# Moving loads, one batch's stores and a store stream around DMA transposes in a fused attention and Fourier-mixing kernel

## The chip, the cores and the metric

The kernel runs on one core of a Trainium2 chip. The metric is device time in microseconds (us): the median of the runs before is 414.62 us (three runs, 414.11 to 414.83). A core has five engines that work through their own instruction lists in order: TensorE (PE in the profile; its weight loads are PEld), VectorE (DVE), ScalarE (ACT), GpSimd (POOL) and SyncE (SP). DMA transfers are issued by an engine's queue and move data while the engines compute; here SP issues the stores and the DMA transposes, POOL the loads.

## The reference

For each of 8 batches and 8 heads, with 576 rows and head dimension 64, the first half is linear attention with exponential features of width 256, and the second half mixes its result along rows and columns with a Fourier transform, normalises, and applies a two-layer network:

```python
def phi(x):
    proj = np.einsum('bhsd,df->bhsf', x, w_phi)
    proj = proj - np.max(np.abs(proj), axis=-1, keepdims=True)
    return np.concatenate([np.exp(proj), np.exp(-proj)], axis=-1)
q_p, k_p = phi(q), phi(k)
kv = np.einsum('bhsf,bhsd->bhfd', k_p, v)
z = np.sum(k_p, axis=2)
attn = np.einsum('bhsf,bhfd->bhsd', q_p, kv) / (np.einsum('bhsf,bhf->bhs', q_p, z)[..., None] + 1e-06)
x = attn, heads joined to (8, 576, 512)
u = x + real(fft over rows and columns of x)
un = (u - mean(u)) / sqrt(var(u) + 1e-06)      # over the 512 columns
out = u + relu(un @ w_ch1) @ w_ch2              # 512 -> 2048 -> 512
```

Inputs and output are float32; the products run in bfloat16.

## The kernel before, in words

Batches are software-pipelined: while the two-layer network of batch b runs, attention and mixing of batch b+1 and the key and query features of batch b+2 are computed between its steps. There is no planner at run time. The order is the string `PLAN` (lines 23 to 37): each letter names a stream, a Python generator that emits some instructions and yields; `step` (line 1345) runs the generator of that letter to its next yield. Every engine executes its instructions in the order in which they are emitted, so the place of a letter fixes the place of its instructions on each engine's list and on each DMA queue.

The streams that matter here, with b the batch:

- `F` (`forward`, line 1200), 68 steps a batch: the network. `hidden(0, 256)` multiplies the first 256 columns of the transposed input `UT` with `W1b` (line 1211, tile `psf`), two 128-row blocks numbered c = 0 and c = 2; `output(c)` multiplies with `W2b` (line 1228, tile `pso`); then `hidden(256, 576)` for blocks 1, 3 and 4. At the end of an `output(c)` DVE adds the result into the tile `X` (line 1234) and the store of block c is issued on SP (`store`, line 1184): one DMA of 256 KB for block 2 and for block 3, four of 128 KB for blocks 0 and 1 together, two for block 4.
- `M` (`mixing`, line 989): per head the key-value product (`keyvalue`, line 842, tile `kv`), `combine` (tile `pn_`, with POOL writing `X` at line 973), then the Fourier mixing, which ends with adds into `X`.
- `N` (`normalise`, line 1100), five steps, blocks in the order 0, 2, 1, 3, 4: DVE takes the statistics (line 1155), ACT writes the centred block `UN` (line 1131), and SP issues a DMA transpose of it into `UT` (line 1148).
- `S` (`scaled`, line 593): POOL multiplies V with its weights, two instructions for each pair of heads (`scale_v`, line 441, tiles `VCn`, `VCp`).
- `K`, `Q`, `V` (lines 1289 to 1309): loads of k, q, v issued on POOL (line 258). `Q` has three steps: four DMAs of 64 KB (`QS01`), one of 256 KB (`QS23`), two for the last block (`QS4`). `K` has two: `KS4` (64 KB) and `KS` (512 KB). `V` has three: two DMAs `VS4` (32 KB each), then two of 256 KB.
- `A` and `B` (`turn_q`, `turn_k`, lines 380 to 398): DMA transposes of q and k on SP, after the loads.

`X` has three buffers; each holds 5 blocks of C + 1 = 513 float32 in every partition, 512 of them used. Three set-up tiles (`gc`, `gs`, `ga`) use the same buffers at the start. The staging tiles of k, q and v have one buffer each, so a load waits until the transposes of the batch before have read the tile.

In the program each tile starts at a multiple of 32 bytes in its partition. A buffer of `X` has 5 x 513 x 4 = 10,260 bytes and takes 10,272; behind the three buffers lie `HT`, `R`, `CEO`, `UN` and `UT`, and `UN` starts at byte 213,408, which is 160 past a multiple of 256.

Of the kernel before, what the change touches and what calls it, by code (L numbers as in the profile page):

```python
# [12 lines left out]
F32 = mybir.dt.float32  # L13
# [9 lines left out]
PLAN = (  # L23
    "CYCCZYCYGGTRTTGZZGTYZWRTJTSRJGRJYSTPTSPKTTPJMJRTSSKMYMBMPTQPTPQVTMZTMQTMMTPCMMMTTMTHDYAMMYHHDHHKYYVD"
    "YDTMTMHTKZMRMSRTYMTTMNYMRVTYQNNMTNTSMNMBFFFRFFNUFNFSMFWFUNRUFQUMTPSFFMNTFPSMTFTNUPYFQMUFPPTVMFTPMTPF"
    "FMMFTTFMFAUTFMMFFMFMFMFMFFKRFPDFFTTTFFDVFFDRFTFFVDFFKTSRFQVFFFFMFFMTFRFFFFFSMTMFFMRTFFMSTMFTFNNMFMQF"
    "PTMMFTFSFMPTFFPTTPMFFFFMFSNBFMFPTQMFFAFMNPFTFMNMFFMFFMMFTTFFURMFFVFRMFFSTFFMFFMFVFTTPFFFFRFPDFFFTPFF"
    "FFFVDDRFFFQFDTMTFFQTSMKFFFMFFFKMRMFTTTMMFNNFFMMFMQFMFFSSMTFMTFFFNFSTPPMFTFMBFPTFPAMFFFMFNTFKMMFFFNFM"
    "FMFFMFFUMQMFFVMFFFTTPFFFFMTFFRFTTFFVFFFRFFRFDFFFFDFDFFDPTFMFTTFFFFMKFRFTMSFMRFFMFTSPMFNTMPQNSFFFFQMM"
    "MMTTTFFBMSFFFFTPMTFSFFMFFMTPVMFFFFMTPNFFNNMMMFFMAFFFMUFMFKMFFFMFFTTDTTFRFFSFFFFRVFFTMFFFFFRPTFFDFFFD"  # L30
    "RFFFTDFMFVKTPFFFFFMTMBQMFFRSFMFTSTSTMMKFFFNNSFMMFMMFTFMFPTMKFFFFPTPMTFFMFFFNMFTPPMFFFTNFQMNMVFFMFQMF"
    "MFFMUFFMFFVMAFFFFTTTTFDRFRFFTFSFFFFMRFFQFFFDFFTFFFDFFRFVDFTFMFFTTMFFMFFMFRSMFQTTTMFTQFNFMSVFFMFFTNPM"
    "MFMSTPMTFFFFSMTPPMFTFFMPPFBAFMFPFMFNNFMMVFMFMFFFMTTFRMNUFFFFFMRFFFMFFFSTFFMFFPTFFTFFFDDFFFRFTFFFDFDV"
    "RFFFMFTTFFMFMTMFRFFSMFFSFMTTNTFFMFNMMFFFMMFTFMPSTFNFFFPTFMFFTMPFFFFMPSPMFFTMFFPFTMNFFFNMFMFFFUMFMFMF"
    "FFFMFFMFMFFFFFDFFDFFFFFDFFFDFMFFFMFMFFMMFFMFNFMNFFFFFFMFFFFFMNFFFMFFNFFFFFFFFFFFFFFFNUFFFFFFFFFFFFFF"
    "FFFFFFFFFFFFFFFFFFFFFFFFFFFFFFFFFFFFF"
)


# [1 line left out]
def kernel(  # L41
# [29 lines left out]
    xpool = ctx.enter_context(tc.tile_pool(name="xpool", bufs=3))  # L71
# [18 lines left out]
    def load_ffn_weights(b):  # L90
# [310 lines left out]
    made, mixed, folds, turned_u, scale_of = {}, {}, {}, {}, {}  # L401
# [493 lines left out]
        yield  # L895

    def first_heads():
        X = xpool.tile([128, 5, C + 1], F32, tag="X", name="X")
        R = fpool.tile([128, 3, 2, 512], F32, tag="R", name="R")
        CEO = fpool.tile([128, 3, 2, 2, 128], BF16, tag="CEO", name="CEO")  # L900
        HI = HIS[0]
        folds[0] = folded(X, R, HI)

        def combine(heads_, ps):
            for e, h in enumerate(heads_):
                for c in range(5):
# [14 lines left out]

        kvh = {}
        for pr in PAIRS:
            for e in range(2):
                kvh[2 * pr + e] = keyvalue(0, 2 * pr + e)
                yield
        for h in (0, 1, 6, 7):
            ps = pb.tile([128, 1, 512], F32, tag="pb", name="pn_")
            combine((h,), ps)
            yield  # L930
        for h in (4, 2):
            ps = pj.tile([128, 2, 512], F32, tag="pj", name="pn_")
            combine((h, h + 1), ps)
            yield
        return X, R, CEO, HI

    def heads(b):
        if b == 0:
            return (yield from first_heads())
        KPp, KPn, K4p, K4n, VCp, VCn, E2 = made[b]  # L940
        X = xpool.tile([128, 5, C + 1], F32, tag="X", name="X")
        R = fpool.tile([128, 3, 2, 512], F32, tag="R", name="R")
        CEO = fpool.tile([128, 3, 2, 2, 128], BF16, tag="CEO", name="CEO")
        HI = HIS[b % 2]
        folds[b] = folded(X, R, HI)

        held = []

        def combine(h, kvh):
            pn_ = pj.tile([128, 2, 512], F32, tag="pj", name="pn_")  # L950
            for c in range(5):
                for i, QP in enumerate((QPHP, QPHN)):
                    nc.tensor.matmul(  # L953
                        pn_[:, i, 65 * c:65 * c + 65], lhsT=QP[:, h, 128 * c:128 * c + 128],
                        rhs=kvh[:, i, :], start=True, stop=True,
                    )
            Av = pn_[:, 0, 0:325].rearrange("p (c n) -> p c n", n=65)
            Bv = pn_[:, 1, 0:325].rearrange("p (c n) -> p c n", n=65)
            tg = work.tile([128, 5, D + 1], F32, tag="tg", name="tg")
            nc.vector.tensor_tensor(  # L960
                out=tg[:], in0=Bv, in1=E2[:, h, :].unsqueeze(2).to_broadcast([128, 5, D + 1]),
                op=ALU.mult,
            )
            if h % 2 == 0:
                held.append(work.tile([128, 2, 5, D + 1], F32, tag="cb", name="cb"))
            cb = held[-1]
            nc.vector.tensor_tensor(out=cb[:, h % 2], in0=Av, in1=tg[:], op=ALU.add)  # L967
            if h % 2 == 0:
                return
            rd = small.tile([128, 2, 5, 1], F32, tag="rd", name="rd")  # L970
            nc.vector.reciprocal(out=rd[:], in_=cb[:, :, :, D:D + 1])  # L971
            at = D * (h - 1)
            nc.gpsimd.tensor_tensor(  # L973
                out=X[:, :, at:at + 2 * D].rearrange("p c (e d) -> p e c d", e=2),
                in0=cb[:, :, :, 0:D], in1=rd[:].to_broadcast([128, 2, 5, D]), op=ALU.mult,
            )
# [223 lines left out]
    def forward(b):  # L1200
        U, UT = turned_u[b]
# [22 lines left out]
        def output(c):  # L1224
            at = PLACE[c]
            po = pb.tile([128, C], F32, tag="pb", name="pso")
            for hh in range(NHH):
                nc.tensor.matmul(  # L1228
                    po[:], lhsT=HT[:, hh, at:at + 128], rhs=W2b[:, hh, :],
                    start=(hh == 0), stop=(hh == NHH - 1),  # L1230
                )
                if hh % 2 and hh < NHH - 1:
                    yield
            nc.vector.scalar_tensor_tensor(  # L1234
                out=U[:, c, 0:C], in0=po[:], scalar=scale_of[b, c], in1=U[:, c, 0:C],
                op0=ALU.mult, op1=ALU.add,
            )
# [22 lines left out]
        for g in range(2):  # L1260
            nc.vector.scalar_tensor_tensor(
                out=U[0:64, 4, 256 * g:256 * g + 256], in0=po[64 * g:64 * g + 64, 0:256],
                scalar=scale_of[b, 4][0:64], in1=U[0:64, 4, 256 * g:256 * g + 256],
                op0=ALU.mult, op1=ALU.add,
            )
        store(b, U, 4)
        yield
        if b < B - 1:
            return
        for at in (0, 256):  # L1270
            po = pb.tile([128, 256], F32, tag="pb", name="pso")
            for hh in range(NHH):
# [58 lines left out]
    def fold_later(b):  # L1331
# [62 lines left out]
```

## Time and profile before

| | |
|---|---|
| median of the runs | 414.62 us (414.11 to 414.83) |
| the profiled execution, its own time | 413.11 us |
| its span, first to last instruction | 411.3 us |
| busy: PE, DVE, ACT, POOL | 390.4, 319.4, 303.6, 214.9 us |
| granted TensorE clock | 0.999 |
| DMA packets moved | 42.71 MB |

Times in the profile count from the start of the span. In a timeline row the columns are: start, length, engine, line, operation, output tile <- input tiles, shapes, number of instructions merged, and in brackets the idle time of the engine just before with what the profile takes to have ended it. A `q` behind an engine's name (`SPq`) marks the issuing of a DMA. A wait for several semaphores is put down to the one that came last by the profile's account.

### The profile page before, as it was taken

The numbers are of one execution on the slowest core, as the hardware profiler recorded it, in microseconds if no ns is written. First come the engines' busy times: TensorE is split into PE (matmuls) and PEld (weight loads), VectorE is DVE, ScalarE is ACT, GpSimd is POOL, SyncE is SP. The second block draws the span as 40 slices with busy tenths as digits, with TensorE's granted clock in tenths as the row PEclk, the third lists the DMA queues.
The fourth block names the chain that finished last, engine by engine and source line by source line (L and its number), as shares of the span: only waits on it lengthen the run. The fifth ranks groups of instructions, "written<-read, shape, count | busy, mean of one in ns | idle before, by whom it ended". The sixth has DMA issues, their size and how long they took to land.

```text
span 411.3 us, 10509 instructions
## 1 busy us (share of the span) xinstructions
PE 390.4 (95%) x4165; PEld 258.7 (63%) x4194; DVE 319.4 (78%) x662; ACT 303.6 (74%) x617; POOL 214.9 (52%) x279
## 2 busy tenths in 40 slices
PE   7898899989999989999899999999999999999995
PEld 3574477535856568566766577556856586657564
DVE  5979887999699877798589888888799768866102
ACT  7988999658958886688868887799768886444350
POOL 8998695774466753807658383649362343201000
PEclk9999999999999999999999999999999999999999
DMA  7999969998574798664964959857782141106202
GB/s 221 218 165 159 184 103 181 88 120 129 101 120 58 68 165 137 77 98 77 137 97 58 155 103 143 88 75 117 114 101 53 33 97 21 26 3 114 60 25 65
DMA packets 108674, 42.71 MB, mean 104 GB/s; under 512 B 82769, under 2 KB 103633, under 8 KB 108625
## 3 DMA queue, kind: packets, MB, share of 16 engines
q0 software_dynamic: 46272, 16.60, 37.3%
q1 hardware_dynamic: 61905, 25.11, 33.2%
q8 instruction: 33, 0.54, 0.5%
q10 hardware_dynamic: 448, 0.33, 0.3%
q14 instruction: 16, 0.13, 0.1%
HBM read 36.77 MB, written 9.44 MB: 112 GB/s over the span
## 4 chain that ended last, share of the span: by engine, by line
PE 77%; DVE 13%; DMA 3%; ACT 3%; POOL 2%; issue 2%; POOLq 0%; DVEq 0%; ACTq 0%
PE psf L1211 30%; PE pso L1228 20%; PE kv L851 4%; PE psD L1033 2%; PE pso L1254 2%; DMA UT<-UN 2%; PE pu L1085 2%; PE idle L1325 2%; PE psq L520 2%; PE psh L561 2%; PE psk L466 1%; DVE cb L967 1%; DVE MK L486 1%; DVE tg L960 1%; DVE R L867 1%
## 5 line engine op out<-in xcount | busy, mean ns | idle before, releaser
L1211 PE MATMUL psf<-UT,W1b 128*128 128x320 bf16 (+1 forms) x1024 | 141.1, 286 | 2.7 <-DVE MQ L528 1.3
L1228 PE MATMUL pso<-W2b,HT 128*128 128x512 bf16 x467 | 117.0, 379 | 1.8 <-issue 0.6
L1211 PEld LDWEIGHTS <-W1b 128*128 128x128 bf16 x1024 | 94.7, 98 | 30.5 <-issue 3.9
L1216 ACT ACTIVATE HT<-psf 128x320 bf16<-128x320 f32 x128 | 53.9, 444 | 25.6 <-PE psf L1211 19.5
L1228 PEld LDWEIGHTS <-HT 128*128 128x128 bf16 x496 | 45.1, 98 | 43.2 <-issue 0.4
L973 POOL TENSOR_TENSOR X<-cb,rd 128x640 f32<-128x640 f32 x28 | 35.1, 1253 | 52.4 <-DVE rd L971 29.5
L441 POOL TENSOR_TENSOR VCn<-VS,VCn 128x512 bf16<-128x512 bf16 x28 | 29.9, 1066 | 43.1 <-ACT VCn L436 36.7
L528 DVE TENSOR_REDUCE MQ<-psq 128x8 f32<-128x1024 f32 (+1 forms) x32 | 34.3, 1088 | 17.3 <-PE psq L520 17.0
L1234 DVE SCALAR_TENSOR_TENSOR X<-pso,rs,X 128x512 f32<-128x512 f32 x31 | 23.0, 743 | 28.2 <-PE pso L1228 28.0
L1218 ACT ACTIVATE HT<-psf 128x512 bf16<-128x512 f32 x64 | 37.3, 602 | 6.4 <-PE psf L1211 6.2
L486 DVE TENSOR_REDUCE MK<-psk 128x8 f32<-128x1024 f32 x28 | 33.8, 1210 | 1.4 <-ACT KPn L472 1.4
L472 ACT ACTIVATE KPp<-psk 128x1024 bf16<-128x1024 f32 x28 | 28.8, 1027 | 7.6 <-PE psk L466 7.5
L258 POOL DMA_DIRECT2D QS<-in_q_dram x49 | 33.4, 687 | 0.9 <-issue 0.9
L1131 ACT ACTIVATE UN<-X,MV 128x512 bf16<-128x512 f32 (+1 forms) x35 | 25.2, 725 | 11.6 <-DVE MV L1156 8.0
L570 ACT ACTIVATE QPHP<-psh 128x1024 bf16<-128x1024 f32 x28 | 28.9, 1031 | 4.7 <-PE psh L561 4.4
L472 ACT ACTIVATE KPn<-psk 128x1024 bf16<-128x1024 f32 x28 | 28.7, 1025 | 1.7 <-DVE MK L486 1.6
L441 POOL TENSOR_TENSOR VCp<-VS,VCp 128x512 bf16<-128x512 bf16 x28 | 29.9, 1067 | 0.0
L570 ACT ACTIVATE QPHN<-psh 128x1024 bf16<-128x1024 f32 x28 | 29.0, 1036 | 0.0
L1155 DVE BATCH_NORM_STATS2 st<-X 128x6 f32<-128x512 f32 (+1 forms) x40 | 27.1, 678 | 0.2
L1075 DVE TENSOR_TENSOR X<-pu,X 128x512 f32<-128x512 f32 (+3 forms) x49 | 23.5, 526 | 4.6 <-PE pu L1085 4.5
L953 PEld LDWEIGHTS <-QPHP 128*128 128x128 bf16 x280 | 20.4, 98 | 7.8 <-DVE cb L967 3.8
L1171 POOL TENSOR_TENSOR rs<-VE,mhalf 128x5 f32<-128x5 f32 (+1 forms) x9 | 10.3, 1147 | 24.8 <-DVE VE L1170 24.7
(462 smaller groups left out, 794.3 us busy)
## 6 DMA issues: line engine op xcount, KB each, us to landing
out_dram<-X SPq DMA_DIRECT2D x16, 256.0 KB
KS<-in_k_dram POOLq DMA_DIRECT2D x7, 512.0 KB, 8.2
VS<-in_v_dram POOLq DMA_DIRECT2D x14, 256.0 KB, 4.8
out_dram<-X SPq DMA_DIRECT2D x28, 128.0 KB
W1b<-in_moe_w_ch_dram POOLq DMA_DIRECT2D x1, 2048.0 KB, 15.6
W2b<-in_moe_w_ch_dram POOLq DMA_DIRECT2D x1, 2048.0 KB, 17.4
QS<-in_q_dram POOLq DMA_DIRECT2D x28, 64.0 KB, 3.6
QS<-in_q_dram POOLq DMA_DIRECT2D x7, 256.0 KB, 5.8
```

What stands on the lines that cost most here:

```text
L258: nc.gpsimd.dma_start(out=pieces[i][0], in_=pieces[i][1])
L441: nc.gpsimd.tensor_tensor(out=VC[:, hs, :, 0:D], in0=values[b][0][:, hs, :].rearrange("p h (j d) -> p h j d", d=D), in1=VC[:, hs, :, D:D + ...
L472: nc.scalar.activation(out=KP[:, hs, :, :].rearrange("p e (jp jj) f -> p jj (e jp) f", jj=2), in_=psk[:], func=AT.Exp, scale=sgn,)
L486: nc.vector.tensor_reduce(out=MK[:, 2 * pr:2 * pr + 2, :].rearrange("p e (jp jj) -> p jj (e jp)", jj=2), in_=tiles[pr][:], axis=AX.X, op=A ...
L528: nc.vector.tensor_reduce(out=o, in_=i[:], axis=AX.X, op=ALU.max, apply_absolute_value=True)
L570: nc.scalar.activation(out=o, in_=psh[:], func=AT.Exp, scale=sgn)
L973: nc.gpsimd.tensor_tensor(out=X[:, :, at:at + 2 * D].rearrange("p c (e d) -> p e c d", e=2), in0=cb[:, :, :, 0:D], in1=rd[:].to_broadcast( ...
L1155: nc.vector.bn_stats(out=st[0:M, :], in_=X[0:M, c, 0:C])
L1211: nc.tensor.matmul(ps, lhsT=W1b[:, cc, 128 * hh:128 * hh + 128], rhs=UT[:, cc, lo:hi], start=(cc == 0), stop=(cc == NCC - 1),)
L1216: nc.scalar.activation(out=HT[:, hh, lo:hi], in_=ps, func=AT.Relu, scale=-1.0)
L1218: nc.scalar.activation(out=HT[:, hh - 1:hh + 1, lo:hi], in_=psw[:].rearrange("p (a n) -> p a n", a=2), func=AT.Relu, scale=-1.0,)
L1228: nc.tensor.matmul(po[:], lhsT=HT[:, hh, at:at + 128], rhs=W2b[:, hh, :], start=(hh == 0), stop=(hh == NHH - 1),)
```

## The change

The change does three things.

First, the stores of batches 0 to 6 leave `forward` and become a stream `O` (`store_all`) of four steps: block 2, blocks 0 and 1, block 3, block 4. `PLAN` gets 28 letters `O`. On SP's list this gives the same order as before in every batch but batch 1: there the four DMAs of blocks 0 and 1 now stand behind the transposes of `UN` blocks 0 and 2 of batch 2 (before: ahead of them), and the DMA of block 3 behind the transpose of block 1 (before: ahead of it).

Second, some load letters move, which changes POOL's list so (all else on it keeps its order):

| load | before | after |
|---|---|---|
| `QS23` of batch 3 (1 DMA) | behind the scalings of pairs 0 and 1, batch 2 | ahead of them |
| `KS4`, `KS` of batch 4 (2 DMAs) | behind `QS23` of batch 4 and the scaling of pair 0, batch 3 | ahead of both |
| `QS4` of batch 4 (2 DMAs) | behind the scaling of pair 0, batch 3 | behind the scaling of pair 3 |
| `QS23` of batch 5 (1 DMA) | ahead of the scaling of pair 1, batch 4 | behind it |
| `KS4` of batch 7 (1 DMA) | ahead of the scaling of pair 3, batch 5 | behind it |
| `VS4` of batch 7 (2 DMAs) | ahead of the scalings of pairs 2 and 3, batch 6 | behind them |

The order of all instructions on PE, ACT and DVE is unchanged.

Third, a block of `X` has 514 elements instead of 513. A buffer then has 10,280 bytes and takes 10,304, so `HT`, `R`, `CEO`, `UN` and `UT` start 3 x 32 = 96 bytes later; `UN` starts at byte 213,504, a multiple of 256.

```diff
 PLAN = (
...
-    "FMMFTTFMFAUTFMMFFMFMFMFMFFKRFPDFFTTTFFDVFFDRFTFFVDFFKTSRFQVFFFFMFFMTFRFFFFFSMTMFFMRTFFMSTMFTFNNMFMQF"
+    "FMMFTTFMFAUTFMMFFMFMFMFMFFKRFPDFFTTTFFDVFFDRFTFFVDFFKTSRFQVFFFFMFOFMTFRFFFFFQSMTMFOFMRTFFMSTMFTFNNMF"
...
-    "FFFVDDRFFFQFDTMTFFQTSMKFFFMFFFKMRMFTTTMMFNNFFMMFMQFMFFSSMTFMTFFFNFSTPPMFTFMBFPTFPAMFFFMFNTFKMMFFFNFM"
+    "FTPFFFFFVDDRFFFQFDTMTFFKKQTSMFFFMFFFMRMFTTTMMFNNOFFMMFMFMFFSSMTFMTFFFNOFOSQTPPMFTFMBFPTFPAMFFFMFNTFK"
...
-        xpool.tile([128, 5, C + 1], F32, tag="X", name=n)[:].rearrange("p a b -> p (a b)")
+        xpool.tile([128, 5, C + 2], F32, tag="X", name=n)[:].rearrange("p a b -> p (a b)")
...
-        X = xpool.tile([128, 5, C + 1], F32, tag="X", name="X")
+        X = xpool.tile([128, 5, C + 2], F32, tag="X", name="X")
...
-            store(b, U, c)
+            if b == B - 1:
+                store(b, U, c)
...
+        if b < B - 1:
+            yield
+            return
         store(b, U, 4)
         yield
-        if b < B - 1:
-            return
...
+    def store_all(b):
+        U = turned_u[b][0]
+        for c in (2, 1, 3, 4):
+            store(b, U, c)
+            yield
...
-        "A": (arrive, 1), "B": (arrive_k, 1), "W": (load_ffn_weights, 2),
+        "A": (arrive, 1), "B": (arrive_k, 1), "O": (store_all, 4), "W": (load_ffn_weights, 2),
```

More of the change, by code (lines that the diff above doesn't have):

```diff
@@ L25 @@
     "YDTMTMHTKZMRMSRTYMTTMNYMRVTYQNNMTNTSMNMBFFFRFFNUFNFSMFWFUNRUFQUMTPSFFMNTFPSMTFTNUPYFQMUFPPTVMFTPMTPF"
-    "FMMFTTFMFAUTFMMFFMFMFMFMFFKRFPDFFTTTFFDVFFDRFTFFVDFFKTSRFQVFFFFMFFMTFRFFFFFSMTMFFMRTFFMSTMFTFNNMFMQF"
-    "PTMMFTFSFMPTFFPTTPMFFFFMFSNBFMFPTQMFFAFMNPFTFMNMFFMFFMMFTTFFURMFFVFRMFFSTFFMFFMFVFTTPFFFFRFPDFFFTPFF"
-    "FFFVDDRFFFQFDTMTFFQTSMKFFFMFFFKMRMFTTTMMFNNFFMMFMQFMFFSSMTFMTFFFNFSTPPMFTFMBFPTFPAMFFFMFNTFKMMFFFNFM"
[L29 to L36, printed above, removed]
+    "FMMFTTFMFAUTFMMFFMFMFMFMFFKRFPDFFTTTFFDVFFDRFTFFVDFFKTSRFQVFFFFMFOFMTFRFFFFFQSMTMFOFMRTFFMSTMFTFNNMF"
+    "MFPTMMFOTFSFMPTFFOPTTPMFFFFMFSNBFMFPTQMFFAFMNPFTFMNMFFMFFMMFTTFFURMFFVFRMFFSTFFMFFMFVFTTPFFOFFRFPDFF"
+    "FTPFFFFFVDDRFFFQFDTMTFFKKQTSMFFFMFFFMRMFTTTMMFNNOFFMMFMFMFFSSMTFMTFFFNOFOSQTPPMFTFMBFPTFPAMFFFMFNTFK"
+    "MMFFFNFMFMFFMFFUMQMFFVMFFFTTPFFFFMTFFRFTTFFOVFFFRFFRFDFFFFDFDFFDPTFMFTTFFFFMKFRFTMSFMRFFOMFTSPMFNTMP"
+    "NSQFFFFQMMMMTTTFFOBMSFFFFOTPMTFSFFMFFMTPVMFFFFMTPNFFNNMMMFFMAFFFMUFMFKMFFFMFFTTDTTFRFFSFFFFRVFFOTMFF"
+    "FFFRPTFFDFFFDRFFFTDFMFVKTPFFFFFMTMBQMFFRSFMFOTSTSTMMFFFNNSFMMFMMFTFMFOPTMKKFFFFOPTPMTFFMFFFNMFTPPMFF"
+    "FTNFQMNMVFFMFQMFMFFMUFFMFFVMAFFFFTTTTFDRFRFFTFSFFFOFMRFFQFFFDFFTFFFDFFRFVDFTFMFFTTMFFMFFMFRSMFOQTTTM"
+    "FTQFNFMSFFMFFTNPMMFOMSTPMTFFFFOSMTPPMFTFFMPPFBAFMFPFMFNNFMMVVFMFMFFFMTTFRMNUFFFFFMRFFFMFFFSTFFMFFPTF"
+    "FOTFFFDDFFFRFTFFFDFDVRFFFMFTTFFMFMTMFRFFSMFFSFOMTTNTFFMFNMMFFFMMFTFOMPSTFNFFFOPTFMFFTMPFFFFMPSPMFFTM"
+    "FFPFTMNFFFNMFMFFFUMFMFMFFFFMFFMFMFFFFOFDFFDFFFFFDFFFDFMFFFMFMFFMMFFMFNFMNFFOFFFFMFFFFOFMNFFFOMFFNFFF"
+    "FFFFFFFFFFFFNUFFFFFFFFFFFFFFFFFFFFFFFFFFFFFFFFFFFFFFFFFFFFFFFFFFF"
 )
@@ L940, in heads @@
         KPp, KPn, K4p, K4n, VCp, VCn, E2 = made[b]
-        X = xpool.tile([128, 5, C + 1], F32, tag="X", name="X")
+        X = xpool.tile([128, 5, C + 2], F32, tag="X", name="X")
         R = fpool.tile([128, 3, 2, 512], F32, tag="R", name="R")
@@ L1362 @@
         for name in STREAMS:
-            assert at_[name] == (1 if name in "WCGZJHY" else B, 0), name
+            assert at_[name] == (1 if name in "WCGZJHY" else B - (name == "O"), 0), name
 _INS = ['q', 'k', 'v', 'w_phi', 'moe_w_ch1', 'moe_w_ch2']
```

## The prediction

> **What bounds the kernel now.** I read the page first, then busy time by stage, the waits of TensorE, and its timeline at each of those waits.
>
> ```profile
> span 411.3 us, 10509 instructions
> PE 390.4 (95%) x4165; PEld 258.7 (63%) x4194; DVE 319.4 (78%) x662; ACT 303.6 (74%) x617; POOL 214.9 (52%) x279
> 77.00:104.00 27.00, 24.75 (x216) 13.27 (x218) 26.30 (x45) 19.12 (x37) 18.04 (x23) 1.00 0.91 112
> 104.00:411.30 307.30, 297.11 (x3100) 200.97 (x3122) 228.57 (x462) 215.98 (x445) 134.97 (x161) 1.00 0.60 87
> ```
>
> The last two lines are stretches of time: length, busy time of PE, PEld, DVE, ACT, POOL, granted clock, DMA share, GB/s. From 77 to 104 us VectorE is the bound (26.30 of 27.00). From 104 us on TensorE is (297.11 of 307.30, with its tail after the last matmul inside). In that stage only what makes TensorE wait is worth time, and little does:
>
> ```profile
> PE psf L1211 <- DVE MQ L528: 1.3, 1, 1.3
> PE psf L1211 <- DMA UT<-UN: 1.2, 2, 1.0
> PE pn__4074 L953 <- DVE MK L486: 0.7, 1, 0.7
> ```
>
> In the timeline the first two rows are three places, each the first matmul of `hidden(0, 256)` of a batch (3, 2 and 5), which needs the transposed blocks 0 and 2:
>
> ```profile
> 150.10 0.19 PE L855 MATMUL kv<-V4N,K4n 128*128 128x65 bf16 x1
> 151.29 0.49 PE L1211 MATMUL psf<-UT,W1b 128*128 128x256 bf16 x3 [1.00 <-DMA UT<-UN]
> 196.43 0.19 PE L855 MATMUL kv<-V4N,K4n 128*128 128x65 bf16 x1
> 197.96 0.49 PE L1211 MATMUL psf<-UT,W1b 128*128 128x256 bf16 x3 [1.34 <-DVE MQ L528]
> 289.80 0.61 PE L1211 MATMUL psf<-UT,W1b 128*128 128x256 bf16 x4 [0.21 <-DMA UT<-UN]
> ```
>
> The second is put down to `MQ` of VectorE, but line 528 reduces `psq`, which from batch 2 on lives in the PSUM pool `pj`, while `psf` takes a buffer of `pb`, and `psf` reads no `MQ`. I take that wait too for the transpose of block 2, which was issued late and moved slowly:
>
> ```profile
> 191.19 3.31 SPq L1148 DMA_TRANSPOSE UT<-UN  x2
> GB/s 178 28 0 0 0 0 0 0 0 72 218 224 201 244 16 0 0 0 0 5 46 53 41 46 36 72 135 172 167 174 164 172 172 166 171 174 176 174 195 171
> 192.34 0.93 POOL L258 DMA_DIRECT2D QS<-in_q_dram  x1 [0.39 <-issue]
> 193.34 1.05 POOL L441 TENSOR_TENSOR VCn<-VS,VCn 128x512 bf16<-128x512 bf16 x1
> 194.36 1.05 POOL L441 TENSOR_TENSOR VCp<-VS,VCp 128x512 bf16<-128x512 bf16 x1
> ```
>
> The second row is what the DMA engines moved in 40 slices from 191 to 197 us (0.15 us each). The first transpose moves at some 220 GB/s, done 2.0 us after its issue; then the 256 KB load of q, issued at 192.34, is in flight, and the rest trickles until TensorE has waited 1.34 us. An undisturbed pair stands in batch 7 (slices of 0.1 us from 369.3):
>
> ```profile
> 369.30 2.73 SPq L1148 DMA_TRANSPOSE UT<-UN  x2
> GB/s 82 0 0 0 0 0 0 0 0 0 0 13 136 223 223 215 223 192 80 8 0 0 0 0 0 0 0 102 212 215 223 223 202 113 21 0 0 0 0 0
> ```
>
> Both have moved by 372.8, 3.5 us after the first issue. From 191.19 that is 194.7, nearly 2 us before TensorE is free (196.43 + 0.19). For batch 2 the SP and POOL rows and the chain say:
>
> ```profile
> 141.61 2.98 SPq L1187 DMA_DIRECT2D out_dram<-X  x4
> 144.91 3.45 SPq L1148 DMA_TRANSPOSE UT<-UN  x2
> 149.40 2.97 SPq L1148 DMA_TRANSPOSE UT<-UN  x1
> 132.22 3.20 POOL L258 DMA_DIRECT2D QS<-in_q_dram  x5
> 138.12 1.05 POOL L441 TENSOR_TENSOR VCn<-VS,VCn 128x512 bf16<-128x512 bf16 x1 [2.70 <-ACT VCp L436]
> 140.14 1.61 POOL L258 DMA_DIRECT2D KS<-in_k_dram  x2
> 141.75 1.44 POOL L258 DMA_DIRECT2D QS<-in_q_dram  x2
> 136.00:141.50 5.50, 5.50 (x36) 3.01 (x35) 4.00 (x8) 4.18 (x12) 3.38 (x4) 1.00 0.52 50
> 141.50:146.30 4.80, 4.75 (x46) 3.04 (x45) 4.40 (x12) 4.38 (x8) 4.03 (x6) 1.00 1.06 110
> 146.36 4.80 DMA UT<-UN
> ```
>
> The DMA engines are full (share 1.06) just as the pair goes out, with half their time free before (0.52). The second transpose lands 4.80 us after its issue (last row, from the chain), at 151.16.
>
> **The change part by part.** *SP's order.* Only batch 1 differs. The four stores (2.98 us of issuing, 512 KB) ended at 144.59, before the transposes could start, so the place in the queue costs nothing today; what goes is 512 KB ahead of them in the DMA rings. Afterwards they stand behind the pair, ahead of block 1, which goes out some 1 to 2 us later than 149.40; so do the k and q transposes behind it.
>
> ```profile
> 163.26 3.26 SPq L1148 DMA_TRANSPOSE UT<-UN  x2
> 171.72 0.98 PE L1211 MATMUL psf<-UT,W1b 128*128 128x320 bf16 x6
> 157.68 0.75 POOL L258 DMA_DIRECT2D KS<-in_k_dram  x1 [7.54 <-DMA KT<-KS]
> 161.08 1.25 POOL L973 TENSOR_TENSOR X<-cb,rd 128x640 f32<-128x640 f32 x1 [2.65 <-DVE rd L971]
> ```
>
> Last of that queue come blocks 3 and 4 (to 166.52), read at 171.72: 5.2 us, less 2 us of moving, cover it. Without that cover it would cost what it is late, 1 to 2 us. A POOL load at 157.68 also waits for the k transposes; `X` behind it has 2.65 us.
>
> *Loads of k and q, batch 4.* Two issues (1.61 us) go ahead of the 256 KB load that ends the group at 135.42, and POOL is then idle 2.70 us: covered. They move their 576 KB in the half-free stretch and are off the rings by about 143. The two `QS4` issues (1.44 us) move to 150.1, into the 7.54 us in which POOL idles. With the stores out of the way too the pair should take 3.5 us from 144.91, so 148.4, before 150.29: gain **1.00**. Uncovered, the 1.61 us would delay the scaling of pair 0 by as much.
>
> *`QS23` of batch 5.* The two scalings of pair 1 start 1 us earlier, the load goes out at about 194.3, and pair 2 behind it keeps its time. Before, its bytes came 1.6 us after the issue, so now from 195.9, after the pair is through: gain **1.34**.
>
> *`VS4` of batch 7, `KS4` of batch 7, `QS23` of batch 3.*
>
> ```profile
> 283.93 1.31 POOL L258 DMA_DIRECT2D VS<-in_v_dram  x2
> 286.10 1.06 POOL L441 TENSOR_TENSOR VCn<-VS,VCn 128x512 bf16<-128x512 bf16 x1 [0.85 <-ACT VCn L436]
> 101.81 1.06 POOL L441 TENSOR_TENSOR VCn<-VS,VCn 128x512 bf16<-128x512 bf16 x1 [5.41 <-ACT VCn L436]
> ```
>
> The first goes out of the way of batch 5's pair: gain **0.21**; the scalings wait for ScalarE anyway. `QS23` of batch 3, an issue of 0.93 us as for batch 5, delays four scalings, with 5.41 us idle behind them; no `psf` wait stands there. One `KS4` passes two scalings: nothing. Each would cost its issue (0.7 to 0.9 us) on POOL if that idle time were gone.
>
> *Rows of 514.* No operation is added. Today's rows start alternately at 0 and 4 bytes past a multiple of 8, and times over all five blocks hardly spread:
>
> ```profile
> L1155 DVE BATCH_NORM_STATS2 st<-X x40: 652/683/696, 52.8 to 377.0; 128x6 f32<-128x512 f32 x32, 64x6 f32<-64x512 f32 x8
> L973 POOL TENSOR_TENSOR X<-cb,rd x28: 1244/1253/1267, 69.9 to 353.8; 128x640 f32<-128x640 f32 x28
> L202 POOL TENSOR_TENSOR ga<-ga,gc 128x512 f32<-128x512 f32 x1 | 1.3, 1262 | 0.1
> ```
>
> I take zero. Bounds: no gain, as no row is quicker by element; at worst POOL writes `X` at the pace of line 202 (1262 / 512 ns an element, 1577 for 640), 0.32 us more each. By the Trainium skill (DMA: Bandwidth & Descriptors, How a descriptor splits into AXI transactions) a read that starts off a 256-byte boundary begins at the boundary below: a 256-byte piece of `UN` at 160 costs 13 beats, at 0 only 8, so by it the pair of transposes would come a few tenths earlier, and the last 0.21 us would go with certainty. No run here shows an aligned `UN` yet, and the sum does without it.
>
> *Sum:* 1.00 + 1.34 + 0.21 = 2.55 us; against its own time 413.11 - 2.55 = 410.56. That execution stands 1.51 us under the median; carried along, **412.1 us**. Bounds of the stalls: nothing, or the whole distance from the `kv` start to the `psf` start in the first two (1.19 + 1.53) and 0.21 = 2.93, so 411.7 at best; I let the low end go half a microsecond further, for waits too short to be listed. Losses are bounded below.
>
> **The rivals.** *(a) One stall goes.* `QS23` is issued at 194.3 and may still hold the pair back, if the pair is itself late. Then 1.34 stays: 414.62 - 1.21 = **413.4**. For it: the first transpose's data was through by 193.3, yet its partner still lost 3 us. By the Trainium skill (DMA: Bandwidth & Descriptors, Queues, rings and completion order) a completion is written only after every earlier write of that DMA engine, across its queues, which would do just this. Against it: 1.2 us between 194.7 and 195.9.
>
> *(b) Given back.* TensorE comes 2.3 us earlier to the wait of 0.7 on `MK`; if what it waits for there hangs on loads, not on TensorE, the gain is returned and 0.21 stays: **414.4**, no change. POOL's `X` there is what would hold it:
>
> ```profile
> 207.87 1.25 POOL L973 TENSOR_TENSOR X<-cb,rd 128x640 f32<-128x640 f32 x1 [5.67 <-DVE rd L971]
> ```
>
> Against it: POOL had idled 5.67 us for a reciprocal that follows TensorE's own products. That the 28 new letters do nothing but for batch 1 is certain from the lists, and is in the sum.
>
> *(c) Slower by the row size.* All 28 writes of `X` at 1577 ns lie on the path through mixing: 9.0 us, 412.1 + 9.0 = **421.1**; it ends slower than before from 8 writes on (8 x 0.32 = 2.56). Against it: the even spread above and POOL's idle time ahead of `X`.
>
> **How the numbers follow.** Forecast 0.60; (a) 0.17; (b) 0.15; (c) 0.08. A measurement here tells about 0.2% (0.83 us) from no change. Forecast and (a) are faster by more: 0.77; (b) is the same: 0.15; (c) slower: 0.08. The range runs from 411.2 to 414.3, up to just short of (b), and leaves out (b)'s middle and (c).
>
> **What would show it.** Right: the three `psf` rows lose their idle time; the pair of batch 2 has landed before the four stores move; POOL's groups `VCn` of batch 4 come back to back ahead of the load; line 973 stays near 1253 ns. Wrong: an idle time of over 0.3 us at a `psf`; a wait on `MK` grown from 0.7 to over 2 us; a PE wait near 171 us for blocks 3 and 4; `X` writes of over 1.4 us.

## The result and the profile after

The median after is 413.36 us (22 runs, 410.92 to 415.57) beside 414.91 us of the kernel before in the same session. The ratio is **0.9939, 95% interval 0.9916 to 0.9961**: 1.6 to 3.5 us faster, and inside the predicted range. The ratio compares undisturbed runs only, so it is not the quotient of the two medians.

The profiled execution of the changed kernel took 413.93 us, more than its median; before, the profiled one (413.11) stood below its median. So the two traces do not show the gain as a shorter span:

```profile
span 412.2 us, 10494 instructions
PE 392.6 (95%) x4165; PEld 260.1 (63%) x4194; DVE 319.9 (78%) x662; ACT 303.6 (74%) x617; POOL 214.5 (52%) x279
```

I therefore cut both traces, and that of a later experiment (`KS4` late, below), at the first `psf` matmul of each batch; the columns are us from one cut to the next.

| from, to | before | after | with `KS4` late |
|---|---|---|---|
| start to batch 0 | 50.40 | 52.08 | 51.10 |
| 0 to 1 | 53.55 | **52.11** | 52.14 |
| 1 to 2 | 47.34 | **46.19** | 46.18 |
| 2 to 3 | 46.67 | **47.00** | **45.16** |
| 3 to 4 | 46.09 | 46.01 | 46.02 |
| 4 to 5 | 45.75 | 45.88 | 45.72 |
| 5 to 6 | 44.23 | **45.59** | 44.24 |
| 6 to 7 | 40.62 | 40.63 | 40.62 |
| 7 to last product | 31.88 | 31.88 | 31.88 |

The first row goes with the granted clock of TensorE, not with the change. The pages give it in 40 equal slices, in tenths (9 is 90% or more), here before and after:

```profile
PEclk9999999999999999999999999999999999999999
PEclk9899899999999999999999999999999999999999
```

In the trace after, two stretches of 3.4 us run at half the clock: 0.51 from 10.8 to 14.2 us and 0.50 from 41.6 to 45.0. Of the 14 traces of this study, five have no such stretch ahead of batch 0's first `psf` and reach it at 50.3 to 50.4 us, four have one (50.8 to 51.1) and five have two (51.9 to 52.2). The rest sums to 356.13, 355.29 and 351.96. Five things happened: 1.44 us gained before batch 1, which I had not foreseen; 1.15 in the stage that ends at batch 2; 1.34 at batch 3, and 1.77 lost ahead of it; 1.36 lost behind batch 5. How the changed kernel's other executions come to the whole measured gain, this one cannot show.

The timeline of TensorE in the changed kernel, at the same places as in the prediction:

```profile
150.34 0.19 PE L855 MATMUL kv<-V4N,K4n 128*128 128x65 bf16 x1
150.38 1.04 PE L1211 MATMUL psf<-UT,W1b 128*128 128x256 bf16 x8
...
197.34 0.19 PE L855 MATMUL kv<-V4N,K4n 128*128 128x65 bf16 x1
197.38 1.36 PE L1211 MATMUL psf<-UT,W1b 128*128 128x256 bf16 x11
...
288.74 0.19 PE L855 MATMUL kv<-V4N,K4n 128*128 128x65 bf16 x1
289.27 1.48 PE L1211 MATMUL psf<-UT,W1b 128*128 128x256 bf16 x12 [0.34 <-DMA UT<-UN]
```

The first two stalls (1.00 and 1.34 us) are gone: `psf` follows `kv` after 0.04 us. The third, 0.21 before, is still there with 0.34. TensorE's waits in the changed kernel (total, times, longest) show two that are new behind the first `psf` (the `psk` row is the wait at 300.63 us), and the one on `MK`, 0.7 before:

```profile
PE pn__3170 L953 <- DVE cb L967: 1.8, 1, 1.8
PE psk L466 <- DMA KT<-KS: 1.4, 1, 1.4
...
PE pn__4074 L953 <- DVE MK L486: 0.6, 1, 0.6
```

**The wait of 1.8 us.** VectorE and POOL in the changed kernel, around 162 us:

```profile
160.79 0.71 POOL L258 DMA_DIRECT2D KS<-in_k_dram  x1 [8.98 <-DMA KT<-KS]
161.51 2.47 POOL L973 TENSOR_TENSOR X<-cb,rd 128x640 f32<-128x640 f32 x2
...
162.07 1.96 DVE L1170 TENSOR_SCALAR VE<-MV 128x5 f32<-128x5 f32 x1
...
165.08 0.20 PE L953 MATMUL pn__3170<-kvh,QPHP 128*128 128x65 bf16 x1 [1.77 <-DVE cb L967]
```

`VE` is an addition on five numbers a partition, 0.12 us at this place in the kernel before. Here it takes 1.96 us and ends 0.05 us after POOL's two writes of `X` (161.51 + 2.47 = 163.98). POOL does both at once because it stood at the load `KS4` of batch 5 until 160.79 (157.68 before), and that load waits for the k transposes of batch 4, which now land 3.1 us later. TensorE waits for VectorE's next `cb`. The Trainium skill (SBUF — State Buffer, SBUF: two separate sides) says that VectorE and GpSimd share one pair of ports, which VectorE needs for some instructions only (in a mode that uses two ports, or with two inputs in SBUF), that whichever instruction starts first holds the pair to its end, and that the other stands still. This trace agrees: `VE` starts 0.56 us into POOL's first write and takes 1.96 us instead of 0.12; that `VE` runs in such a mode no run here shows. A held `VE` need not cost anything: the one near 256 takes 1.21 us in every trace that has it on VectorE, the kernel before included, and the stage around it (4 to 5) is no shorter with it on ScalarE (45.76 in `ve_act` below, 45.72 with `KS4` late).

**The 1.44 us before batch 1** are the same thing the other way round. The kernel before, VectorE and POOL:

```profile
90.91 1.25 POOL L441 TENSOR_TENSOR VCn<-VS,VCn 128x512 bf16<-128x512 bf16 x1
92.13 1.36 POOL L441 TENSOR_TENSOR VCp<-VS,VCp 128x512 bf16<-128x512 bf16 x1
...
90.70 1.88 DVE L1005 TENSOR_TENSOR CEO<-R 128x381 bf16<-128x381 f32 x2
92.50 1.03 DVE L1051 CAST CEO<-R 128x6 bf16<-128x6 f32 x1
...
92.64 0.55 PE L1033 MATMUL psD<-CS,CEO 128*128 128x289 bf16 x3 [1.15 <-DVE CEO L1005]
```

The kernel after:

```profile
92.49 0.94 POOL L258 DMA_DIRECT2D QS<-in_q_dram  x1
93.49 1.06 POOL L441 TENSOR_TENSOR VCn<-VS,VCn 128x512 bf16<-128x512 bf16 x1
...
92.37 1.02 DVE L1005 TENSOR_TENSOR CEO<-R 128x381 bf16<-128x381 f32 x2
93.31 0.17 DVE L1051 CAST CEO<-R 128x6 bf16<-128x6 f32 x1
...
93.45 0.92 PE L1033 MATMUL psD<-CS,CEO 128*128 128x289 bf16 x6 [0.29 <-DVE CEO L1005]
```

With `QS23` of batch 3 ahead of them, POOL's scalings start after these VectorE steps instead of beside them: 1.88 + 1.03 us become 1.02 + 0.17, in the stage that VectorE bounds. No run moved this load alone. But of the 14 traces the six with the load in its old place have 1.02 or 1.03 us at L1051 and 40.86 to 40.87 us from the second half of batch 0's `psf` to batch 1's, and the eight with it moved have 0.17 or 0.18 and 39.42 to 39.44. The rows of 514, the only other part of the change that reaches that stage, are in the first set too (the run with them alone).

### The profile page after: what moved, and what is told of

Same layout as the page of the kernel before. It is cut to its first block, busy times and chain, and to the rows that moved or that the text cites. A ratio compares the mean times of both kernels' runs of the same rounds, so it can differ in the third digit from the quotient of the medians.

```text
span 412.2 us, 10494 instructions
## 1 busy us (share of the span) xinstructions
PE 392.6 (95%) x4165; PEld 260.1 (63%) x4194; DVE 319.9 (78%) x662; ACT 303.6 (74%) x617; POOL 214.5 (52%) x279
## 4 chain that ended last, share of the span: by engine, by line
PE 76%; DVE 16%; DMA 3%; POOL 2%; issue 1%; ACT 1%; DVEq 0%; POOLq 0%
PE psf L1211 29%; PE pso L1228 20%; PE kv L851 4%; PE pso L1255 3%; PE psD L1033 2%; DMA KT<-KS 2%; PE pu L1085 2%; PE psh L561 2%; PE psk L466 2%; PE psq L520 2%; DVE R L867 2%; DVE MK L486 1%; DVE cb L967 1%; PE idle L1333 1%; DVE tg L960 1%
## 5 line engine op out<-in xcount | busy, mean ns | idle before, releaser
L973 POOL TENSOR_TENSOR X<-cb,rd 128x640 f32<-128x640 f32 x28 | 35.1, 1254 | 46.4 <-DVE rd L971 19.5
```

The costliest lines, as they stand in the source:

```text
L973: nc.gpsimd.tensor_tensor(out=X[:, :, at:at + 2 * D].rearrange("p c (e d) -> p e c d", e=2), in0=cb[:, :, :, 0:D], in1=rd[:].to_broadcast( ...
```

## The experiments

Queue lists are given in short: st1.c1 is the store of block 1 (with 0) of batch 1, UT2.c0 the transpose of block 0 of batch 2, VC0 the scaling of pair 0. "Lands" is the last completion of a DMA in the trace, counted from its issue where a length is given.

**Which part frees which pair.** Three kernels make one part of the change each in the kernel before; the fourth takes a part of it back.

```diff
 batch2_part: SP's list, and POOL's loads of batch 4
-st1.c1 x4, UT2.c0, UT2.c2, st1.c3, UT2.c1
+UT2.c0, UT2.c2, st1.c1 x4, UT2.c1, st1.c3
-QS23, VC0, KS4, KS, QS4 x2, VC1, VC2, VC3
+KS4, KS, QS23, VC0, VC1, VC2, VC3, QS4 x2
```

> The kernel before with only the batch 2 part of the change: the stores of batch 1 behind the transposes, KS4 and KS of batch 4 earlier, QS4 of batch 4 later; rows of 513. Theory T (bytes in flight beside the transposes hold them back): the psf of batch 2 loses its 1.00 us, the one of batch 3 keeps its 1.3 us; the k transposes of batch 4 land about 3 us later than before (160 instead of 157), POOL's X comes at 161.5 instead of 161.1, meets VectorE's VE (L1170), which then takes about 2 us, and TensorE waits 1.5 to 2 us near 165 as in the changed kernel: time 0.5 to 1 us above the kernel before less 0, so within 1 us of it. Rival P (the 1.77 us near 165 in the changed kernel was an accident of that one execution, not of the order): VE takes 0.12 us, nothing near 165, time 1.0 us below. Rival R (the stalls go by the rows of 514): psf of batch 2 still waits 1.0 us.

Ratio 0.9988 (0.9967 to 1.001). The stall at batch 2 is gone and the one at batch 3 stays; near 165 the new wait is there again:

```profile
150.06 0.19 PE L855 MATMUL kv<-V4N,K4n 128*128 128x65 bf16 x1
150.09 1.04 PE L1211 MATMUL psf<-UT,W1b 128*128 128x256 bf16 x8
...
161.79 1.42 DVE L1170 TENSOR_SCALAR VE<-MV 128x5 f32<-128x5 f32 x1
...
164.27 0.20 PE L953 MATMUL pn__3170<-kvh,QPHP 128*128 128x65 bf16 x1 [1.24 <-DVE cb L967]
```

So this part gives 1.0 us and takes 1.24 back; the `psf` of batch 4, which had not waited before, waits 0.51 us in this trace. `KT4` of batch 4 landed at 160.61, as theory T has it; rival P, an accident of one execution, falls.

```diff
 qs23_only: POOL's list, batch 5's load and batch 4's scalings
-QS23, VC1
+VC1, QS23
```

> The kernel before with only QS23 of batch 5 moved behind the scalings of pair 1; rows of 513. Theory T: the psf of batch 3 loses 1.2 to 1.4 us of its 1.34, that of batch 2 keeps 1.00; the k transposes of batch 5 land up to 2 us later without a TensorE wait; time 1.3 us below the kernel before (ratio 0.997). Rival R (rows of 514 do it): psf of batch 3 still waits 1.3 us, ratio 1.000.

Ratio 0.9975 (0.9947 to 1.0004). The transpose of block 2 of batch 3 lands in 2.93 us (5.09 before) and the stall is gone; that of block 0 still takes 4.00 (4.35 before), so the load of q was not all that held the pair. The stall of batch 2 stays with 1.16:

```profile
153.21 0.49 PE L1211 MATMUL psf<-UT,W1b 128*128 128x256 bf16 x3 [1.16 <-DMA UT<-UN]
...
198.36 0.19 PE L855 MATMUL kv<-V4N,K4n 128*128 128x65 bf16 x1
198.39 1.47 PE L1211 MATMUL psf<-UT,W1b 128*128 128x256 bf16 x12
```

```diff
 rows514_only (the set-up tiles gc, gs and ga alike)
-        X = xpool.tile([128, 5, C + 1], F32, tag="X", name="X")
+        X = xpool.tile([128, 5, C + 2], F32, tag="X", name="X")
```

> The kernel before with rows of 514 and nothing else. Theory T: all three psf waits stay (1.0, 1.3, 0.2 us), undisturbed transposes land 0.1 us sooner (2.3 instead of 2.4 us after their issue), time the same (ratio 0.999 to 1.001). Rival R (the start of UN at a multiple of 256 bytes cuts the transposes' packets): the psf waits of batches 2 and 3 shrink by more than half and the time falls by 1 to 2.5 us.

Ratio 1.0007 (0.9972 to 1.0043); both large stalls stay (the third is 0.06 us in this trace, 0.21 before), and POOL's writes of `X` keep their 1253 ns:

```profile
153.08 0.60 PE L1211 MATMUL psf<-UT,W1b 128*128 128x256 bf16 x4 [1.28 <-DMA UT<-UN]
...
199.80 0.38 PE L1211 MATMUL psf<-UT,W1b 128*128 128x256 bf16 x2 [1.41 <-DVE MQ L528]
...
L973 POOL TENSOR_TENSOR X<-cb,rd 128x640 f32<-128x640 f32 x28 | 35.1, 1253 | 52.1 <-DVE rd L971 29.5 <-DVE VE L1170 14.9 <-issue 7.5
```

Undisturbed transposes (batch 7) land in 2.28 and 2.33 us instead of 2.42: the start at a multiple of 256 bytes is worth 0.1 us each, far from the two large stalls.

```diff
 vs4_back: POOL's list in the changed kernel, batch 7's load and batch 6's scalings
-VC2, VC3, MQ, VS4 x2, VS
+VS4 x2, VC2, VC3, MQ, VS
```

> The changed kernel with the two loads VS4 of batch 7 back ahead of the scalings of pairs 2 and 3 of batch 6. Theory T: the k transposes of batch 7 land about 2 us sooner (298.3 instead of 300.6) and the 1.38 us that TensorE waited for them near 300 go; the psf of batch 5 still waits 0.2 to 0.4 us: 1.0 to 1.4 us below the changed kernel (about 412.0 where that has 413.4; ratio to the kernel before 0.990 to 0.993). Rival: the wait near 300 has another cause (the instruction load that stands at 298.8 in the DMA records), and stays at 1.4 us; time as the changed kernel, 413.4.

Ratio 0.9932 (0.9899 to 0.9965), 412.52 us: not clearly below the changed kernel. The wait near 300 is gone, with the first of the two large k transposes landing at 299.67 instead of 300.58; but the wait near 165 was larger in this trace:

```profile
161.98 2.69 DVE L1170 TENSOR_SCALAR VE<-MV 128x5 f32<-128x5 f32 x1
...
165.72 0.20 PE L953 MATMUL pn__3170<-kvh,QPHP 128*128 128x65 bf16 x1 [2.50 <-DVE cb L967]
...
299.44 0.41 PE L452 MATMUL ps<-wphi,KT 64*64 64x128 bf16 x8
299.78 0.40 PE L466 MATMUL psk<-wphi,KT 64*128 64x128 bf16 x8
```

**Stores or loads at batch 2.** The two edits of the first experiment, one at a time in the kernel before.

> The kernel before with only the stores of batch 1 behind the transposes; the loads of k and q stay as before, rows of 513. Theory S (the 512 KB of stores ahead of the pair are what held it): the transposes of UN of batch 2 land within 2.5 us of their issue (before 5.88 and 4.80), the 1.00 us at the psf of batch 2 goes. Rival L (the loads KS and QS4 issued at 140 to 143 held it): the pair still needs over 4 us and the wait stays above 0.7 us. For the wait near 165 (1.40 with stores and loads moved together): if the stores behind the pair delay the k transposes of batch 4, KT4 lands at 159 or later and TensorE still waits over 1 us near 165; if the two QS4 loads at 150 do, KT4 lands near 157 and nothing is lost near 165, time 1.0 us below the kernel before (ratio 0.9976).

> The kernel before with only KS4 and KS of batch 4 issued earlier and QS4 of batch 4 later; the stores of batch 1 stay ahead of the transposes, rows of 513. Theory S: the pair of batch 2 still needs over 4 us and its psf still waits 0.7 us or more. Rival L: the pair lands within 3 us, the wait goes. Near 165: if QS4 at 150 delays the k transposes of batch 4, KT4 lands at 159 or later (before 157.1) and TensorE waits over 1 us near 165, time 1 to 1.5 us above the kernel before; if the stores do, nothing is lost there.

Stores alone, ratio 0.9981 (0.9955 to 1.0006):

```profile
150.03 0.19 PE L855 MATMUL kv<-V4N,K4n 128*128 128x65 bf16 x1
150.06 1.04 PE L1211 MATMUL psf<-UT,W1b 128*128 128x256 bf16 x8
...
161.75 1.87 DVE L1170 TENSOR_SCALAR VE<-MV 128x5 f32<-128x5 f32 x1
...
164.68 0.20 PE L953 MATMUL pn__3170<-kvh,QPHP 128*128 128x65 bf16 x1 [1.69 <-DVE cb L967]
```

Loads alone, ratio 0.9957 (0.9932 to 0.9982):

```profile
151.71 0.19 PE L855 MATMUL kv<-V4N,K4n 128*128 128x65 bf16 x1
151.74 1.04 PE L1211 MATMUL psf<-UT,W1b 128*128 128x256 bf16 x8
...
163.43 0.12 DVE L1170 TENSOR_SCALAR VE<-MV 128x5 f32<-128x5 f32 x1
```

Either alone ends the stall, so neither S nor L is right as stated. The loads do more: the pair lands in 2.81 and 2.44 us with them, in 4.65 and 3.68 with the stores, just in time. And the stores carry the cost: behind the pair they hold up what follows. Counted from the last `kv` product ahead of batch 2's first `psf`, `KT4` of batch 4 lands after 10.9 us with the stores moved (160.97 - 150.03), after 8.1 with the loads alone (159.79 - 151.71), where `VE` gets through ahead of POOL's second write, and after 7.0 in the kernel before (157.10 - 150.10).

One more thing moves with these loads: TensorE's own instruction loads, which a later experiment shows to slow transposes (`fetch_shift` below). In the four traces with the loads of batch 4 in their old place one of them starts 2.1 to 2.7 us after the pair's first issue, while the pair is under way (146.96 with the stores alone, issue at 144.83). In the ten with these loads moved it starts within 0.7 us of that issue (146.50 and 146.51 with the loads alone) or clear of the pair. Part of what the loads' move gives may be this; no run separates the two.

**Through POOL, or straight.** Two ways to break the chain from the late k transposes to the wait near 165, both with `VS4` back (`eps_` is a constant column of 1e-06; lines behind it are numbered 2 higher):

```diff
 ks4_late: POOL's list, batch 5's load
-QS4 x2, KS4, X, X
+QS4 x2, X, X, KS4
 ve_act: L1170, from batch 1 on
-nc.vector.tensor_single_scalar(out=VE[:], in_=mv[:, cs, 1], scalar=1e-06, op=ALU.add)
+nc.scalar.activation(out=VE[:], in_=mv[:, cs, 1], func=AT.Identity, bias=eps_, scale=1.0)
```

> The changed kernel with VS4 of batch 7 back (as in the run before) and with the load KS4 of batch 5 issued behind POOL's first two X writes of batch 3 instead of ahead of them. Theory C (POOL stands at that load until the k transposes of batch 4 have landed, its X writes come late and together, and VectorE's VE of L1170 is held while POOL works on them): X is written at about 160.0 and 162.5, VE takes 0.12 us, the 2.5 us that TensorE waited near 165 are gone; time 2 us below the run before this one: 410.5 (ratio to the kernel before 0.987 to 0.990). Rival (the wait near 165 comes from the transposes' traffic itself, not through POOL): TensorE still loses over 1 us near 165, time 412.5.

> The changed kernel with VS4 of batch 7 back, and VE = MV + 1e-06 (L1170) computed by ScalarE instead of VectorE from batch 1 on; POOL's load and X writes stay where they were. Theory C: POOL's X writes still come late and together near 162, but VectorE goes straight on to its next products, and the wait near 165 falls from 2.5 us to 0.5 or less; time 411 (ratio 0.988 to 0.992). Rival C2 (any VectorE work is held while POOL writes X late, or TensorE waits for X itself): a VectorE operation after the one taken away is stretched to 1 us or more, TensorE still loses over 1 us there; time 412.5.

`KS4` late: **409.69 us, ratio 0.9862 (0.9828 to 0.9897)**. `VE` on ScalarE: 409.61 us, 0.986 (0.9825 to 0.9894). With `KS4` late the two writes of `X` come apart and `VE` stands between them:

```profile
159.20 1.25 POOL L973 TENSOR_TENSOR X<-cb,rd 128x640 f32<-128x640 f32 x1 [8.35 <-DVE rd L971]
161.27 1.25 POOL L973 TENSOR_TENSOR X<-cb,rd 128x640 f32<-128x640 f32 x1 [0.82 <-DVE VE L1170]
162.47 0.74 POOL L258 DMA_DIRECT2D KS<-in_k_dram  x1
...
161.11 0.12 DVE L1170 TENSOR_SCALAR VE<-MV 128x5 f32<-128x5 f32 x1
```

In the other kernel POOL is as late as ever (its load at 160.08, both writes from 160.80 on), and yet:

```profile
162.10 0.50 DVE L969 TENSOR_TENSOR cb<-pn__3127,tg 128x325 f32<-128x325 f32 x1 [0.72 <-POOL X L975]
...
162.66 0.20 PE L955 MATMUL pn__3171<-kvh,QPHP 128*128 128x65 bf16 x1 [0.48 <-DVE cb L969]
```

What is left, 0.48 us, is that `cb` waits for the first `X` itself. So theory C holds: the cost lay in one tiny VectorE instruction that met POOL's writes.

**Are the stores worth moving, and what holds batch 5's pair?** All three start from the kernel with `KS4` late.

```diff
 stores_back: SP's list
-UT2.c0, UT2.c2, st1.c1 x4, UT2.c1, st1.c3
+st1.c1 x4, UT2.c0, UT2.c2, st1.c3, UT2.c1
 stores5_behind: SP's list
-st4.c1 x4, UT5.c0, UT5.c2
+UT5.c0, UT5.c2, st4.c1 x4
 fetch_shift: the idle products of the start
-            for x in range(4):
+            for x in range(8):
...
-                    ps[:], lhsT=ones_b[:], rhs=ones_b[:].unsqueeze(1).to_broadcast([128, 4, 128]),
+                    ps[:, 0:256], lhsT=ones_b[:], rhs=ones_b[:].unsqueeze(1).to_broadcast([128, 2, 128]),
```

The idle products are products at the start whose results nobody reads; cut in halves, they are the same work in twice the instructions.

> The kernel of the run with KS4 of batch 5 late, and in it the stores of batch 1 back ahead of the transposes of UN blocks 0 and 2 of batch 2 (SP's order as in the kernel before; the loads stay moved). Theory (either move alone frees the pair, so the stores' move adds nothing): the psf of batch 2 waits 0.1 us or less, KT4 of batch 4 lands no later than with the stores moved (158.9), time the same within 0.3 us of that run (409.7; ratio to the kernel before 0.985 to 0.988). Rival (the store move is what carries the gain): the psf of batch 2 waits 0.7 us or more and the time is 1 us higher.

> The kernel with KS4 of batch 5 late, and in it the four stores of blocks 0 and 1 of batch 4 behind the transposes of UN blocks 0 and 2 of batch 5 (the move that the change made for batch 1). Theory T (bytes ahead of the pair in the rings): the pair lands within 3 us of its issue (3.75 and 4.00 us before), the 0.2 to 0.5 us that the psf of batch 5 waited in every run so far are gone, time 0.2 to 0.4 us lower than 409.7; the k transposes of batch 7 land later by up to 3 us and may take 1 us back near 297. Rival I (the instruction load of 16 KB that stands at 284.2, within the pair's move, holds its last part): the pair still lands about 4 us after its issue, wait unchanged.

> The kernel with KS4 of batch 5 late, and the idle products that keep TensorE's clock up at the start cut in halves (120 of 256 columns for 60 of 512), so that TensorE's instruction list is 120 instructions longer before all that follows and its loads of 16 KB come some 60 products, about 4 to 5 us, earlier against the transposes of UN. Rival I (instruction loads in flight hold the transposes): the first transposes of batches 3 and 4 and both of batch 5, which had such a load within their move and needed 3.8 to 4.1 us, now land 2.3 to 3.0 us after their issue, and the psf of batch 5 waits 0.1 us or less. Theory T (only the stores and loads of data count): they still need 3.8 to 4.1 us and the wait stays at 0.2 to 0.5 us. Time 409.7 either way within 0.4 us.

Stores back: 409.69 us, ratio 0.9878 (0.9847 to 0.991), the same as with the stores moved; `psf` of batch 2 follows `kv` after 0.03 us, and `KT4` lands 2.4 us sooner (156.49 beside 158.94; 1.7 us of it counted from that `kv` product). The store stream, the largest edit of the change, adds nothing.

Batch 4's stores behind batch 5's pair: 416.02 us, ratio 1.0007 (0.9976 to 1.0038), 6 us lost against its own base. The second transpose still lands in 4.03 us and the wait stays (0.20), so theory T falls there. And the k transposes pay; behind the wait of 4.15 us TensorE's granted clock is 0.50 from 299.6 to 306.4 us, so that the stage loses 7.2 us (51.48 beside 44.24 with `KS4` late):

```profile
286.26 1.48 PE L1211 MATMUL psf<-UT,W1b 128*128 128x256 bf16 x12 [0.20 <-DMA UT<-UN]
300.05 0.63 PE L452 MATMUL ps<-wphi,KT 64*64 64x128 bf16 x8 [4.15 <-DMA KT<-KS]
```

The longer instruction list: 412.2 us, ratio 0.9926 (0.989 to 0.9962). The page counts TensorE's instruction loads as a queue of their own, 33 of 16 KB (the same in the kernels before and after):

```profile
q8 instruction: 33, 0.54, 0.5%
```

Their starts in the DMA records move against the transposes, and the transposes follow. Each cell: us to landing for blocks 0 and 2, and the start of the load that falls into the pair's move, if one does. `ks4_late` is the base of `fetch_shift`, `stores_back` that of `combined`.

| pair of batch | ks4_late | stores_back | fetch_shift | combined (below) |
|---|---|---|---|---|
| 3 | 3.90, 2.76 (191.00) | 3.87, 2.75 (190.26) | 2.33, 2.32 | 2.32, 2.33 |
| 4 | 2.35, 3.34 (237.54) | 4.18, 3.34 (236.49) | 2.36, 2.32 | 2.38, 2.31 |
| 5 | 3.75, 4.00 (284.22) | 3.61, 3.98 (283.23) | 4.25, 3.01 | 4.85, 3.59 (282.20) |
| 6 | 2.40, 2.28 | 2.40, 2.29 | 2.39, 2.31 | 2.39, **3.96** (327.75) |
| 7 | 2.30, 2.34 | 2.29, 2.33 | 2.30, 2.33 | 2.29, 2.33 |

Rival I holds for batches 3 and 4, whose pairs now land as fast as the undisturbed one of batch 7. At batch 5 the wait is gone (0.03 us from `kv` to `psf`), but the first transpose takes 4.25 us with no such load in its move; what holds it, bytes of the other transfers perhaps, no run tests alone. The loads have only moved elsewhere: one from 165.54 (2.03 us long) meets the transposes of blocks 3 and 4 of batch 2, block 3 takes 6.02 us, and TensorE waits. Behind that wait its granted clock is 0.50 from 171.8 to 175.2 us, and the stage from batch 2 to batch 3 takes 49.27 us instead of 45.16, more than was won:

```profile
171.55 0.77 PE L1211 MATMUL psf<-UT,W1b 128*128 128x320 bf16 x3 [2.01 <-DMA UT<-UN]
```

**All together:** stores back, `KS4` late, `VE` on ScalarE, and half of that shift (64 instructions).

> The kernel with KS4 of batch 5 late and the stores of batch 1 back ahead of the transposes, and in it two more things: VE of L1170 on ScalarE from batch 1 on, and 8 of the 15 groups of idle products at the start cut in halves, so that TensorE's instruction list is 64 instructions (32 products) longer and its loads of 16 KB come about 2 to 3 us earlier against the transposes of UN. Theory I (such loads hold the transposes they meet): the load of batch 5 starts near 280.5 instead of 283.2, so the second transpose of batch 5 lands 2.3 to 3.2 us after its issue (3.98 without the shift) and the 0.2 us at its psf go; no load falls on the transposes of blocks 3 and 4 of batch 2 near 163 (as with the shift twice as large), so no wait near 171. Theory C (VE held by POOL's writes of X): the VE that took 1.2 us near 252 is gone from VectorE. Time 409.2 to 409.7, the same as without the two or 0.1% lower. Rival: both places stay, or a new wait of over 0.5 us appears where a shifted load meets other transposes; time 410 to 412.

410.01 us, ratio 0.9864 (0.9819 to 0.991): no better than without the two additions. The wait at batch 5 and the long `VE` are gone, and a load now falls on the pair of batch 6 (last column of the table), for 0.2 us; near 296 TensorE waits 0.48 us for k transposes. The fastest kernels of the study are thus the three at 409.6 to 409.7 us: by the ratios 1.2 to 1.4% below the kernel before and 0.6 to 0.8% below the changed one.

## Why the prediction was right, and where it was not

The total was right (412.1 of 414.62 is a ratio of 0.9939), its make-up only in half.

- **Stall of batch 2, 1.00 us: right.** It went in every kernel with either edit, and the pair landed 3.65 us after its first issue (forecast 3.5). That either edit alone suffices fits full rings as the reason; how much of the stall was an instruction load that fell into the pair's move stays open. That both edits were needed was not claimed, and they are not.
- **Stall of batch 3, 1.34 us: right**, with one load as its cause (`qs23_only`), and the profile's "DVE MQ" as its misnomer: for block 2, 5.09 us to landing became 2.93. Block 0 stays at 3.8 to 4.0 us until an instruction load leaves it (2.33 in `fetch_shift`); the forecast did not have that load. Rival (a) would have kept it; the trace after has 2.80 us.
- **Stall of batch 5, 0.21 us: wrong.** The step that took `VS4` as its cause failed: the stall stayed at 0.34, and is 0.28 with `VS4` back in its old place (`vs4_back`). In the 12 traces where a 16 KB instruction load starts 3.4 to 3.9 us after that pair's first issue it is 0.06 to 0.42 us; it is nothing only in `fetch_shift`, with no such load in the pair's move, and in `combined`, with one 2.0 us after the issue. I had not looked at that queue.
- **"`QS23` of batch 3 ... no `psf` wait stands there", costed at nothing: wrong by 1.4 us of gain.** I counted POOL's queue and idle time, not what POOL's scalings did to VectorE beside them, in the one stage that I had said VectorE bounds.
- **"`X` behind it has 2.65 us" against "1 to 2 us late": mis-sized.** The k transposes of batch 4 landed 3.1 us later. The cover was used up, and the price of 1.77 us was for the most part not the lateness itself but the held `VE`: with `VE` on ScalarE 0.48 us is left. The wait that I had bounded, on blocks 3 and 4 near 171, did not come.
- **`VS4` of batch 7: the scalings had cover, the transposes did not.** Three loads now go out together at 290, beside the k transposes of batch 7; with them back the 1.38 us near 300 were gone.
- **Rows of 514: right**, zero. Rival (c) falls with 1254 ns at L973. What I had drawn from the Trainium skill's rule on beats (DMA: Bandwidth & Descriptors, How a descriptor splits into AXI transactions), that the last 0.21 us would go with certainty, was too strong: an undisturbed transpose lands 0.1 us sooner, and the stall is 0.06 us in `rows514_only` but 0.34 in the changed kernel.
- **Rival (b): refuted.** The wait on `MK` is 0.6 to 0.7 us in every trace; gains were given back, but at two other places.

So 1.00 and 1.34 were earned as forecast, 1.44 came unasked, and 1.77 and 1.36 were paid unasked: the size of the sum owes something to chance.

## What to carry to other kernels

Before moving a load or a store, list what waits for each transfer that will now fly beside it, not only for the one to be freed: here three of the moves (the stores, the loads of batch 4, `VS4` of batch 7) put a delay on k transposes. When POOL computes, look at what VectorE does in the same microsecond: a tiny instruction that takes ten times its usual time (largest against median of a line) is the sign, though whether TensorE pays for it has to be read from its waits; moving one load out of that meeting (ratio 0.9932 to 0.9862) was worth as much as the whole change. Undo each part of a winning change alone; its largest part may be the one that gives nothing.

## What was unexpected of the hardware

- VectorE and POOL hold each other: 0.12 us became 1.4 to 2.7 us (`VE`, four traces), 0.17 became 1.03 (`CAST`), and POOL's scalings 1.36 instead of 1.05 us. In three of these four, `VE` is recorded as starting 0.1 to 0.6 us before the writes of `X`, while POOL still issued its load; so the issue of a load may hold it too, which no run here tests alone.
- TensorE's instruction loads (16 KB about every 125 products, some 1 us each) delay DMA transposes that are under way by 0.4 to 1.8 us (2.33 us to landing became 2.75 to 4.18). That they share the DMA engines is inferred; that the place of the load decides is shown by the two kernels with longer lists.
- TensorE's granted clock falls to half for 3.4 us at a time: none, one or two such stretches ahead of the first `psf` make 50.3, 51 or 52 us of it, whatever the kernel. They also follow two of the long waits, those of 4.15 us (`stores5_behind`, 6.8 us at half clock) and 2.01 us (`fetch_shift`, 3.4 us), which so cost more than their length; the wait of 2.50 us in `vs4_back` has none behind it.
